# Attention and a routed FFN on one core: token rows scattered to expert regions batch by batch

## The chip, the core and the metric

The kernel runs on one core of one Trainium2 chip. The core has a matrix engine (TensorE, PE in the profile), a vector engine (DVE), a scalar engine (ACT), GpSimd (POOL) and a sync engine (SP) that mostly issues transfers. Each engine runs its own instructions in order and waits on semaphores for the others. The metric is the time of one execution in device microseconds (us), as a median over runs.

## The reference

The computation has two halves. Blockwise causal attention runs on q, k and v of 8 batches, 8 heads, 576 positions and 64 columns, with blocks of 64: a position sees its own block and all earlier ones. The heads are joined to x of 8 x 576 rows of 512. Then each row goes through one of 8 experts:

```
for s in range(S):
    fresh_e = argmax(logits[b, s])            # logits = x @ w_gate
    e = fresh_e if s == 0 or local_gate[b, s] < 0.5 else prev_e
    prev_e = e
    p = softmax(logits[b, s])
    out[b, s] = p[e] * (relu(x[b, s] @ w1[e]) @ w2[e])
```

The local gate is a sigmoid of x @ w_local. The expert of a token so depends on the token before it, within its batch: a scan along the sequence. w1 is 512 x 1024 and w2 is 1024 x 512 for each expert.

## The kernel before

Attention goes over 32 head pairs, four for each batch. Its loop (L607) is software pipelined: pass i turns the probabilities of pair i (`turn_p`, L519, PE transposes L526, evacuated by ACT or DVE at L541), makes scores of pair i + 1 (`scores`, L492) with row maxima on DVE (L508) and exponentials on ACT (L516), transposes q and k of pair i + 2 (`turn`, L471 to L478), finishes pair i - 1 (`finish`, L569), and multiplies by v (`attend`, L553). `pin` keeps the instructions of an engine in the order of the program. Loads are issued by SP for pair i + 3, except k of the first two pairs, which ACT issues; the columns of w_gate and w_local are loaded into `wg` from ACT's queue as well (L459, L460). `inverse` (L560) makes the inverse row sums `rv` by six DVE reciprocals. `finish` multiplies the attention output by `wg`, which holds an identity and the gate columns, so one matmul (L578) gives rows of x and their logits; DVE scales both by `rv`; POOL adds the logits into `lg_all` (L590, L591); SP writes the rows of x to HBM as `x_rows` (L593, L594). POOL also issues the loads of the expert weights, 16 of 1 MB, one after the other behind certain pairs.

`routing` (L145) is a generator. `routing(0)` handles batches 0 to 5 and takes one step at fixed points of pairs 24 to 31:

```
MIDDLE = {25: 1, 28: 1, 29: 1, 30: 1, 31: 2}
BEHIND = {24: 1, 25: 1, 26: 1, 27: 1, 28: 1, 29: 1, 30: 1, 31: 2}
```

Its steps: the argmax; a PE transpose (L188) and a round trip through HBM that lays the tokens of a batch in a row (L191, L193); the scan (L202); the way back (L204, L206, matmul L210); one-hot experts; ranks by matmuls with a triangular and a full matrix of ones (L225); the number of 128-token tiles of each expert; and, for each batch, one-hot matrices of slots (`hot`, L330, five POOL multiplies at L343) multiplied on PE (`add`, L350) to invert "token to slot" into tables: the token numbers that a tile gathers (`tok_g`), those that it writes (`tok_s`) and the probabilities (`pslot`). Steps left over at pair 31 run after the loop.

The FFN has 43 tiles of 128 tokens, each of one expert: 20 from the first six batches and 23 for all that is left. `gather` (L665, POOL) fetches rows of `x_rows` by `tok_g` with a bounds check; `turn_x` (L674) transposes them, DVE evacuates (`xb`, L677); `fetch` (L691) copies the expert's w1 into `wt` on DVE; `up` (L700) multiplies, with relu on ACT (L707) or, for the second half of a tile from tile 18 on, on DVE (L709); `down` (L714) multiplies by w2; ACT scales by the probability (L719); and POOL scatters the rows to the output (L720) with a bounds check. In program order tile t + 1's `up` is ahead of tile t's `down`. `routing(1)` repeats the routing for the last two batches and builds the tables of the last 23 tiles from all eight, one step per tile, on DVE.

## Time and profile before

| what | us |
|---|---|
| median of 3 runs (624.21 to 625.07) | 624.47 |
| the profiled execution | 625.85 |
| its span in the trace | 623.8 |
| PE busy | 563.6 |
| DVE busy | 452.7 |
| ACT busy | 329.4 |
| POOL busy | 155.3 |
| one head pair, pairs 2 to 24 | 11.90 |
| first up matmul of the FFN at | 429.81 |
| last tile's up matmuls at | 605.23 |

Times inside the trace count from the start of the span. The mean clock granted to PE was 0.975 of full speed. The costliest single groups are the exponentials (L516, 158.3 us on ACT), the row maxima (L508, 134.5 us on DVE) and the probability transposes (L526, 105.1 us on PE). A line such as "12.34 0.49 DVE L478 COPY kT<-ps_t" reads: start, duration, engine, line of the kernel, operation, output and input; what stands in brackets is the engine's idle time before it and what ended it.

### The profile page before, as it was taken

The page shows a single profiled execution, that of the slowest core. Times are in us where ns is not written, and L with a number is a line of the kernel's source. Part 1 is how long each engine was busy: PE and PEld are TensorE (multiplying, and loading weights), DVE is VectorE, ACT ScalarE, POOL GpSimd, SP SyncE. Part 2 cuts the span into 40 slices and gives each one's busy share as a digit, 9 for nine tenths or more (in the row PEclk, how much of TensorE's full clock was granted, in tenths as well). Part 3 has the DMA queues.
Part 4 walks back from the last instruction along what each step waited for, and adds up shares of the span by engine and source line. Part 5 has one row for each costly group of instructions (what it writes and reads, how often), then busy time and mean ns, then how long its engine had stood idle before and what let it go on. Part 6 is the DMA issues. An engine that isn't in the chain of part 4 may idle for free. (4 is left out here: it accounts for less than half of the span.)

```text
span 623.8 us, 15804 instructions
## 1 busy us (share of the span) xinstructions
PE 563.6 (90%) x5586; PEld 396.2 (64%) x5586; DVE 452.7 (73%) x1403; ACT 329.4 (53%) x1057; POOL 155.3 (25%) x218
## 2 busy tenths in 40 slices
PE   2899999999999999999999998765989899999991
PEld 1567667677677677666766665554667677766660
DVE  1688888888888888888888788894588855555540
ACT  1676676666666676666666765601444343323320
POOL 3000010010000001001010010144565565666532
PEclk9999999999999999999999999986999999999996
DMA  8246596595958668695874746102232222222210
GB/s 165 55 96 115 116 158 117 120 177 102 170 123 158 103 131 163 114 182 109 153 136 96 136 90 113 23 10 61 78 104 77 99 89 78 94 91 90 82 56 0
DMA packets 154078, 65.99 MB, mean 106 GB/s; under 512 B 138010, under 2 KB 146226, under 8 KB 154002
## 3 DMA queue, kind: packets, MB, share of 16 engines
q0 software_dynamic: 18048, 31.86, 24.8%
q1 hardware_dynamic: 132466, 32.52, 24.2%
q10 hardware_dynamic: 3488, 0.61, 0.6%
q8 instruction: 46, 0.75, 0.5%
q14 instruction: 30, 0.25, 0.1%
HBM read 67.55 MB, written 16.02 MB: 134 GB/s over the span
## 5 line engine op out<-in xcount | busy, mean ns | idle before, releaser
L516 ACT ACTIVATE pb<-ps_s,nm 128x512 f32<-128x512 f32 (+4 forms) x320 | 158.3, 501 | 97.8 <-DVE nm L508 97.3
L508 DVE TENSOR_REDUCE nm<-ps_s 128x1 f32<-128x512 f32 (+4 forms) x320 | 134.5, 453 | 54.0 <-ACT pb L516 31.8
L526 PE MATMUL ps_p<-id_f,pb 128*128 128x128 f32 (+1 forms) x800 | 105.1, 282 | 11.4 <-ACT pb L516 8.0
L492 PE MATMUL ps_s<-kT,qT 64*64 64x512 f32 (+7 forms) x1280 | 100.7, 419 | 6.1 <-ACT qT L475 6.1
L526 PEld LDWEIGHTS ps_p<-id_f,pb 128*128 128x128 f32 (+1 forms) x800 | 86.3, 141 | 24.7 <-ACT pb L516 10.0
L590 POOL TENSOR_TENSOR tmp<-tmp 128x45 f32<-128x45 f32 x32 | 8.5, 264 | 356.9 <-DVE tmp L582 356.9
L700 PEld LDWEIGHTS <-wt 128*128 128x128 bf16 x1376 | 81.1, 98 | 21.1 <-issue 15.8
L553 PE MATMUL ps_o<-pt,vt 128*64 128x320 f32 (+4 forms) x896 | 93.6, 360 | 0.0
L700 PE MATMUL ps_h<-xb,wt 128*128 128x128 bf16 x1376 | 84.3, 220 | 9.3 <-DVE xb L677 9.1
L714 PE MATMUL ps_o<-w_bf,hT 128*128 x344 | 86.6, 379 | 0.4
L553 PEld LDWEIGHTS ps_o<-pt,vt 128*64 128x64 f32 x896 | 59.3, 137 | 35.8 <-DVE tmp L582 4.9
L707 ACT ACTIVATE hT<-ps_h 128x512 bf16<-128x512 f32 x61 | 36.4, 597 | 79.1 <-PE ps_h L700 79.1
L720 POOL DMA_INDIRECT out_dram<-o_sb,tok_s x43 | 54.5, 1268 | 63.8 <-DMA out_dram<-o_sb,tok_s 21.0
L492 PEld LDWEIGHTS ps_s<-kT,qT 64*64 64x64 f32 x1280 | 45.4, 134 | 38.2 <-issue 23.6
L691 DVE COPY wt<-w_bf 128x4096 bf16 x43 | 53.1, 1238 | 15.5 <-PE ps_h L700 13.0
L516 ACT ACTIVATION_READ_ACCUMULATOR pb<-ps_s,nm 128x1 f32 x320 | 64.3, 201 | 0.0
L665 POOL DMA_INDIRECT xg<-x_rows,tok_g x43 | 55.3, 1286 | 22.6 <-PE ps_x L674 9.3
L719 ACT ACTIVATE o_sb<-ps_o,pslot 128x512 f32<-128x512 f32 x43 | 29.5, 687 | 44.0 <-PE ps_o L714 38.3
L709 DVE TENSOR_SCALAR hT<-ps_h 128x512 bf16<-128x512 f32 x25 | 17.3, 691 | 48.1 <-PE ps_h L700 48.1
L578 PE MATMUL ps_n<-wg,ot 128*128 128x146 f32 x320 | 49.4, 303 | 0.0
L541 ACT COPY pt<-ps_p 64x128 f32<-64x128 f32 (+2 forms) x102 | 43.6, 441 | 10.5 <-PE ps_p L526 10.3
L714 PEld LDWEIGHTS <-hT 128*128 128x128 bf16 x344 | 31.2, 98 | 24.8 <-issue 1.1
(147 smaller groups left out, 568.7 us busy)
## 6 DMA issues: line engine op xcount, KB each, us to landing
w_bf<-in_moe_w_dram POOLq DMA_DIRECT2D x16, 1024.0 KB, 10.2
natq<-in_q_dram SPq DMA_DIRECT2D x64, 128.0 KB, 2.6
vt<-in_v_dram SPq DMA_DIRECT2D x64, 128.0 KB, 4.7
natk<-in_k_dram SPq DMA_DIRECT2D x60, 128.0 KB, 2.7
x_rows<-xt SPq DMA_DIRECT2D x32, 128.0 KB, 2.6
natq<-in_q_dram SPq DMA_DIRECT2D x32, 32.0 KB, 2.5
vt<-in_v_dram SPq DMA_DIRECT2D x32, 32.0 KB, 6.3
natk<-in_k_dram SPq DMA_DIRECT2D x30, 32.0 KB, 2.2
```

Of the source, the lines that this page charges most:

```text
L492: pin(nc.tensor.matmul(ps[y][f * 64:(f + 1) * 64, c:c + n], lhsT=qT[r, i * 64:(i + 1) * 64], rhs=kT[r, a:a + n], start=True, stop=True))
L508: pin(nc.vector.reduce_max(nm[:, z:z + 1], ps[g][y][:, c:c + n], axis=AX, negate=True))
L516: pin(nc.scalar.activation(pb[i][:, a:a + n], ps[g][y][:, c:c + n], func=AF.Exp, bias=nm[:, i:i + 1], accum_out=rs[:, z:z + 1]))
L526: pin(nc.tensor.transpose(ps[:kk, (c + e) * P:(c + e + 1) * P], pb[i0 + 2 * e][:, j * P:j * P + kk], id128))
L541: pin(cp(dst, src))
L553: pin(nc.tensor.matmul(ps[h * D:(h + 1) * D, a - q0:qn], lhsT=vts[i % 3][:, j, h, :], rhs=pt[j][:, h, a - j * P:a - j * P + n], start=(j = ...
L578: pin(nc.tensor.matmul(ps[:, (t - t0) * (P + WG):(t - t0 + 1) * (P + WG)], lhsT=ot[:, t * P:(t + 1) * P], rhs=wg[:, hp], start=True, stop= ...
L665: nc.gpsimd.indirect_dma_start(out=xg[:], out_offset=None, in_=x_dram[:rows], in_offset=bass.IndirectOffsetOnAxis(ap=tok_gs[k][:, u:u + 1] ...
L691: nc.vector.tensor_copy(wt.rearrange("p k f -> p (k f)"), w1_bf[:, bass.ds(o, WE)])
L700: nc.tensor.matmul(ps_h[:, f, :], lhsT=wt[:, ko, fo * P:(fo + 1) * P], rhs=xb[:, ko * P:(ko + 1) * P], start=(ko == 0), stop=(ko == KO1 - 1))
L714: nc.tensor.matmul(ps_o, lhsT=hT[:, fo, :], rhs=w2_bf[:, bass.ds(woff + fo * Dm, Dm)], start=(fo == 0), stop=(fo == FO - 1))
L720: nc.gpsimd.indirect_dma_start(out=out_flat, out_offset=bass.IndirectOffsetOnAxis(ap=tok_ss[k][:, u:u + 1], axis=0), in_=o_sb[:], in_offse ...
```

## The change

- Rows are kept per batch in SBUF, as 258 words: 512 bf16 values of x, the token's number and its probability. After a batch's routing, five indirect transfers scatter them to `x_sorted`, where each expert owns a region of 4608 rows. Each transfer writes through a view of its own, declared disjoint from the others. Rows past the end of a batch go to spare rows.
- `routing(b)` now handles one batch and has eight steps, at (pair, part) points given by `hook`: part 0 is after the transposes of the probabilities, 1 before the third group of scores, 2 at the end of a pass. Batches 0 to 6 run inside attention, batch 7 in the FFN. A running count `K.free` gives each expert's next free row.
- The tables come from the counts alone (`table`): `table(0)` for 16 tiles in pair 28, `table(1)` for 27 tiles in the FFN. Slots, one-hot inversions, `tok_s` and `pslot` are gone; the token's number and probability come with the gathered row.
- Three tiles are gathered at the end of pass 29, the other 13 of the first part behind the last pair's gate logits.
- Gathers have no bounds check; output scatters write through disjoint views and have one only for the last seven tiles.
- One DVE reciprocal and six POOL copies take the place of six reciprocals; `wg` and k of pair 1 are loaded by SP; a one-element exponential stands at the start of ACT; v has two buffers for three and is loaded for pair i + 2 instead of i + 3; the evacuations of the probabilities have one pattern for all pairs; DVE takes the second relu from tile 14 on.

The diff, cut to its core:

```diff
-    lg_all = w_p.tile([P, B * NJ, E + 1], F32, tag="lg_all", name="lg_all")
-    x_dram = nc.dram_tensor("x_rows", [BS, Dm], BF16).ap()
+    ROW = Dm // 2 + 2
+    xs = nc.dram_tensor("x_sorted", [E * BS + B * P, ROW], I32).ap()
+    xs_views = dram_disjoint_views(xs, B * NJ)
+    out_views = dram_disjoint_views(out_flat, NT)
+    PARTS = [NB0 * S // P - E - 3, 0]
+    PARTS[1] = NT - PARTS[0]
...
+    TILES = [(k, u) for k in range(2) for u in range(PARTS[k])]
+    def gather(t, xg):
+        k, u = TILES[t]
+        nc.gpsimd.indirect_dma_start(
+            out=xg[:], out_offset=None, in_=xs,
+            in_offset=bass.IndirectOffsetOnAxis(ap=rows[k][:, u:u + 1], axis=0))
+        return xg
+    EARLY = 3
+    xgs = []
+    def gather_early():
+        for t in range(EARLY):
+            xgs.append(gather(t, rt([P, ROW], I32, "x_first", bufs=EARLY)))
+    def new_batch():
+        x = rt([P, NJ, ROW], I32, "x_b", bufs=2)
+        lg = rt([P, NJ, E + 1], F32, "lg", bufs=2)
+        return x, lg
+    def routing(b, x, lg, psum, pin, ew):
+        full = [P, NJ, E]
+        mx = rt([P, NJ], F32, "mx")
+        pin(dve.reduce_max(mx, lg[:, :, :E], axis=AX))
+        mx3 = mx[:, :, None].to_broadcast(full)
+        eqm = rt(full, F32, "eqm")
+        pin(dve.tensor_tensor(eqm, lg[:, :, :E], mx3, op=ALU.is_ge))
+        pin(ew.tensor_mul(eqm, eqm, K.desc[:, None, :].to_broadcast(full)))
+        ep = rt(full, F32, "ep")
+        pin(ew.tensor_sub(ep, lg[:, :, :E], mx3))
+        pin(pool.iota(x[:, :, Dm // 2:Dm // 2 + 1], pattern=[[P, NJ], [0, 1]],
+                      base=b * S, channel_multiplier=1))
+        yield
+        best = rt([P, NJ], F32, "best")
+        pin(dve.reduce_max(best, eqm, axis=AX))
+        ak = rt([P, 2, NJ], F32, "ak")
+        pin(dve.tensor_single_scalar(ak[:, 1, :], lg[:, :, E], 0.0, op=ALU.is_ge))
+        pin(dve.memset(ak[0:1, 1, 0:1], 0.0))
+        fresh = rt([P, NJ], F32, "fresh")
+        pin(dve.tensor_scalar(fresh, ak[:, 1, :], -1.0, 1.0, op0=ALU.mult, op1=ALU.add))
+        pin(dve.scalar_tensor_tensor(ak[:, 0, :], best, -float(E), fresh,
+                                     op0=ALU.add, op1=ALU.mult))
+        pin(nc.scalar.activation(ep, ep, func=AF.Exp))
+        yield
+        ps = psum()
+        pin(nc.tensor.transpose(ps[:2 * NJ, :P], ak.rearrange("p a c -> p (a c)"), id_f))
+        akT = rt([2 * NJ, P], BF16, "akT")
+        pin(nc.scalar.copy(akT, ps[:2 * NJ, :P]))
+        a_dram = nc.dram_tensor("a_dram%d" % b, [2, NJ * P], BF16).ap()
+        nc.sync.dma_start(out=a_dram.rearrange("a (t p) -> (a t) p", p=P), in_=akT)
+        row = rt([1, 2, NJ * P], BF16, "row")
+        nc.sync.dma_start(out=row, in_=a_dram.rearrange("(o a) s -> o a s", o=1))
+        sm = rt([P, NJ], F32, "sm")
+        pin(dve.reduce_sum(sm, ep, axis=AX))
+        yield
+        pin(dve.reciprocal(sm, sm))
+        pin(dve.tensor_tensor_scan(row[:, 0, :S], row[:, 1, :S], row[:, 0, :S], 0.0,
+                                   op0=ALU.mult, op1=ALU.add))
+        e_dram = nc.dram_tensor("e_dram%d" % b, [1, NJ * P], BF16).ap()
+        nc.sync.dma_start(out=e_dram, in_=row[:, 0, :])
+        ecr = rt([NJ, P], BF16, "ecr")
+        nc.sync.dma_start(out=ecr, in_=e_dram.rearrange("o (t p) -> (o t) p", p=P))
+        yield
+        ps = psum()
+        pin(nc.tensor.matmul(ps[:, :NJ], lhsT=ecr, rhs=K.id_b[:NJ, :NJ], start=True, stop=True))
+        oh = rt(full, BF16, "oh")
+        pin(dve.tensor_tensor(oh, ps[:, :NJ, None].to_broadcast(full),
+                              K.niota[:, None, :].to_broadcast(full), op=ALU.is_equal))
+        pin(dve.memset(oh[64:, NJ - 1:, :], 0.0))
+        cum = rt([P, NJ + 1, E], BF16, "cum")
+        pin(ew.memset(cum[:, 0:1, :], 0.0))
+        for c in range(NJ):
+            pin(ew.tensor_add(cum[:, c + 1, :], cum[:, c, :], oh[:, c, :]))
+        pin(ew.tensor_mul(ep, ep, oh))
+        yield
+        ps = psum()
+        n = NJ * E
+        pin(nc.tensor.matmul(ps[:, :n], lhsT=K.tri_b, rhs=oh.rearrange("p c e -> p (c e)"),
+                             start=True, stop=False))
+        pin(nc.tensor.matmul(ps[:, :n], lhsT=K.ones_b,
+                             rhs=cum[:, :NJ].rearrange("p c e -> p (c e)"),
+                             start=False, stop=True))
+        pin(nc.tensor.matmul(ps[:, n:n + E], lhsT=K.ones_b, rhs=cum[:, NJ, :],
+                             start=True, stop=True))
+        rk = rt([P, NJ + 1, E], F32, "rk")
+        pin(nc.scalar.copy(rk.rearrange("p c e -> p (c e)"), ps[:, :n + E]))
+        pg = rt([P, NJ], F32, "pg")
+        pin(dve.reduce_sum(pg, ep, axis=AX))
+        pin(dve.tensor_mul(x.bitcast(F32)[:, :, Dm // 2 + 1], pg, sm))
+        yield
+        pin(dve.tensor_add(rk[:, :NJ], rk[:, :NJ], K.free[:, None, :].to_broadcast(full)))
+        pin(dve.tensor_mul(rk[:, :NJ], rk[:, :NJ], oh))
+        to = rt([P, NJ], F32, "to")
+        pin(dve.reduce_sum(to, rk[:, :NJ], axis=AX))
+        to_i = rt([P, NJ], I32, "to_i", bufs=2)
+        pin(dve.tensor_copy(to_i, to))
+        pin(dve.tensor_copy(to_i[64:, NJ - 1:], K.spare[64:, b:b + 1]))
+        pin(dve.tensor_add(K.free, K.free, rk[:, NJ]))
+        yield
+        for c in range(NJ):
+            pin(pool.indirect_dma_start(
+                out=xs_views[b * NJ + c], out_offset=bass.IndirectOffsetOnAxis(ap=to_i[:, c:c + 1], axis=0),
+                in_=x[:, c, :], in_offset=None))
+        yield
+    def table(k, pin):
+        nt = PARTS[k]
...
+        pin(dve.tensor_sub(cnt, K.free, K.first))
+        if k == 1:
+            pin(dve.tensor_sub(cnt, cnt, K.taken))
+            ts(cnt, cnt, 1.0, float(P - 1))
+        pin(dve.tensor_copy(ci[:, 0], cnt))
+        pin(dve.tensor_single_scalar(ci[:, 1], ci[:, 0], 7, op=ALU.arith_shift_right))
+        pin(dve.tensor_copy(til, ci[:, 1]))
+        pin(dve.tensor_tensor_scan(end, K.ones_e, til, 0.0, op0=ALU.mult, op1=ALU.add))
+        pin(dve.tensor_sub(exc, end, til))
+        ts(a, exc, -float(P), K.part[:, 0:1])
+        pin(dve.tensor_add(a, a, K.first))
+        yield
+        no = rt([P, nt], F32, "no")
         if k == 0:
+            pin(dve.tensor_copy(no, K.tile_no[:, :nt]))
+            lim = small("lim")
...
+        else:
+            pin(dve.tensor_add(a, a, K.taken))
+            last = rt([P, 1], F32, "last")
+            ts(last, end[:, E - 1:], 1.0, -1.0)
...
+            pin(dve.tensor_scalar(no, K.tile_no[:, :nt], last[:, 0:1], 0.0,
+                                  op0=ALU.min, op1=ALU.add))
...
+        ge = rt(full, F32, "ge", tag="big")
+        pin(dve.tensor_tensor(ge, no[:, :, None].to_broadcast(full),
+                              end[:, None, :].to_broadcast(full), op=ALU.is_ge))
+        te = rt([1, nt], F32, "te")
+        pin(dve.reduce_sum(te, ge[0:1], axis=AX))
+        ts(te_is[k], te, float(WE), 0.0)
+        yield
+        prod = rt(full, F32, "prod", tag="prod")
+        def pick(out, f, name):
+            d = small(name)
+            pin(dve.memset(d[:, E - 1:], 0.0))
+            pin(dve.tensor_sub(d[:, :E - 1], f[:, 1:], f[:, :E - 1]))
+            pin(dve.tensor_mul(prod, ge, d[:, None, :].to_broadcast(full)))
+            pin(dve.reduce_sum(out, prod, axis=AX))
+            ts(out, out, f[:, 0:1], 0.0, op0=ALU.add)
+        r = rt([P, nt], F32, "r")
+        pick(r, a, "d_a")
+        pin(dve.scalar_tensor_tensor(r, no, float(P), r, op0=ALU.mult, op1=ALU.add))
+        if k == 1:
...
+            pin(dve.tensor_tensor(r, r, rc, op=ALU.min))
+        pin(dve.tensor_copy(rows[k], r))
...
-        vts = [cst.tile([P, NJ, 2, D], F32, tag="v%d" % x, name="vt") for x in range(3)]
+        vts = [cst.tile([P, NJ, 2, D], F32, tag="v%d" % x, name="vt") for x in range(2)]
...
-                eng = nc.scalar if nm == "k" and i < 2 else nc.sync
+                eng = nc.scalar if nm == "k" and i == 0 else nc.sync
...
+        warm = rt([P, 1], F32, "warm")
+        nc.vector.memset(warm, 0.0)
+        pin(nc.scalar.activation(warm, warm, func=AF.Exp))
...
-            nc.scalar.dma_start(out=wg[r, :, c:c + E], in_=gsrc[h])
-            nc.scalar.dma_start(out=wg[r, :, c + E:c + E + 1], in_=lsrc[h])
+            nc.sync.dma_start(out=wg[r, :, c:c + E], in_=gsrc[h])
+            nc.sync.dma_start(out=wg[r, :, c + E:c + E + 1], in_=lsrc[h])
...
+            pin(nc.vector.reciprocal(rs[:, :NB], rs[:, :NB]))
             for f in range(2):
                 r = slice(f * 64, (f + 1) * 64)
-                pin(nc.vector.reciprocal(rv[:64, 0:1, f ^ swap[0]], rs[r, 0:1]))
-                pin(nc.vector.reciprocal(rv[:64, 1:, f ^ swap[2]], rs[r, 2:NB:2]))
-                pin(nc.vector.reciprocal(rv[64:, :NJ - 1, f ^ swap[1]], rs[r, 1:NB:2]))
+                pin(nc.gpsimd.tensor_copy(rv[:64, 0:1, f ^ swap[0]], rs[r, 0:1]))
+                pin(nc.gpsimd.tensor_copy(rv[:64, 1:, f ^ swap[2]], rs[r, 2:NB:2]))
+                pin(nc.gpsimd.tensor_copy(rv[64:, :NJ - 1, f ^ swap[1]], rs[r, 1:NB:2]))
...
-            r = x_dram[b * S:(b + 1) * S, hp * P:(hp + 1) * P]
-            nc.sync.dma_start(out=r[:S4].rearrange("(t p) d -> p t d", p=P), in_=xt[:, 0:4, :])
-            nc.sync.dma_start(out=r[S4:], in_=xt[:S - S4, 4, :])
+            first, second = tmp[:, :, 0], tmp[:, :, 1]
+            last = pin(nc.gpsimd.tensor_add(lg if hp == 0 else first, first, second))
+            if hp > 0:
+                last = pin(nc.gpsimd.tensor_add(lg, lg, first))
...
+        def plan(steps, at):
+            for a in at:
+                todo.setdefault(a, []).append(steps)
+        def hook(i, part):
+            if part == 2 and i % HP == 0 and i > 0:
+                b = i // HP - 1
+                steps[b] = routing(b, *batches[b], psum, pin, pool)
+                plan(steps[b], [(i, 2), (i + 1, 0), (i + 1, 1), (i + 2, 0), (i + 2, 2),
+                                (i + 3, 1), (i + 3, 2), (i + 3, 2)])
+                if b == NB0 - 1:
+                    plan(table(0, pin), [(i + 4, 0), (i + 4, 1), (i + 4, 2)])
+            for x in reversed(todo.get((i, part), ())):
+                next(x, None)
+            if (i, part) == (HP * NB0 + HP + 1, 2):
+                gather_early()
...
-                engines = ("dve", "act", "dve", "act", "act", "act" if 24 < i < 31 else "dve", "act")
-                for u, eng in enumerate(engines):
+                for u, eng in enumerate(("dve", "act", "dve", "act", "act", "dve", "act")):
                     turn_p(u, eng)
+            hook(i, 0)
...
-            for _ in range(MIDDLE.get(i, 0)):
-                next(steps)
+            hook(i, 1)
...
-                attend(i, 1)
+                pv_last = attend(i, 1)
                 inverse(rss[i])
             if i + 3 < NPR:
-                nats[i + 3] = load(i + 3)
-            for _ in range(BEHIND.get(i, 0)):
-                next(steps)
-        for _ in steps:
-            pass
-        finish(NPR - 1)
+                nats[i + 3] = load(i + 3, "qk")
+            if i + 2 < NPR and i >= 0:
+                load(i + 2, "v")
+            hook(i, 2)
+        gate_last = finish(NPR - 1)
...
-            if n == 0 or t < NT0 - 2:
+            if n == 0 or t < N0 - 2:
...
+            tok = xgs[t][:, Dm // 2:Dm // 2 + 1]
+            if t >= NCT:
+                tok_e = f_p.tile([P, 1], I32, tag="tok_e", name="tok_e")
+                nc.gpsimd.tensor_tensor(tok_e, tok, skip_i[:, t - NCT:t - NCT + 1], op=ALU.add)
+                tok = tok_e
...
             nc.gpsimd.indirect_dma_start(
+                out=out_views[t],
+                out_offset=bass.IndirectOffsetOnAxis(ap=tok, axis=0),
+                **({"bounds_check": BS - 1, "oob_is_err": False} if t >= NCT else {}))
...
+        def gather_next():
+            t = len(xgs)
+            xgs.append(gather(t, x_p.tile([P, ROW], I32, tag="xg", name="xg")))
+        with tc.issue_after(gate_last.ins):
+            while len(xgs) < N0:
+                gather_next()
...
+        def late_steps():
+            for b in range(NB0, B):
+                if b not in steps:
+                    steps[b] = routing(b, *batches[b], psum, lambda x: x, dve)
+                yield from steps[b]
+            yield from table(1, lambda x: x)
+        late = late_steps()
...
+                with tc.issue_after(pv_last.ins):
+                    xb = turn_x(xgs[t])
...
-            for _ in range(1 if t < 8 or t % 2 else 2):
-                next(steps, None)
-            if t + ahead < NT:
-                xgs.append(gather(t + ahead))
+            for _ in range(2 if t < 6 else 1):
+                next(late, None)
+            while len(xgs) < min(NT, t + ahead + 1):
+                if len(xgs) == N0:
+                    for _ in late:
+                        pass
+                gather_next()
```

## The prediction

> **What bounds the kernel now.** I read the slices of the page first, then the busy times by stretch with one stretch per head pair, then the timeline at each joint. Page, slices of the span (digits are tenths):
>
> ```profile
> PE   2899999999999999999999998765989899999991
> DVE  1688888888888888888888788894588855555540
> PEclk9999999999999999999999999986999999999996
> ```
>
> PE is full but for the start, a dip around slices 25–28 and the end: the end is set by PE plus these gaps. Stretches (busy time and instructions by engine, granted clock, DMA):
>
> ```profile
> core 0: us, PE busy (x) PEld busy (x) DVE busy (x) ACT busy (x) POOL busy (x), PEclk, DMA share, GB/s
> 201.14:213.04 11.90, 11.90 (x117) 8.31 (x113) 10.02 (x36) 8.02 (x29) 1.40 (x3) 1.00 0.47 90
> ...
> 332.70:345.44 12.74, 12.21 (x114) 8.29 (x114) 9.77 (x34) 9.18 (x35) 1.44 (x3) 1.00 0.41 84
> ...
> 358.47:372.22 13.75, 12.37 (x116) 8.42 (x116) 11.04 (x40) 8.72 (x32) 2.10 (x4) 1.00 0.41 76
> ...
> 386.81:401.91 15.10, 12.49 (x103) 8.59 (x104) 12.80 (x44) 8.25 (x31) 2.13 (x7) 0.89 0.37 63
> ...
> 411.10:429.81 18.71, 5.51 (x38) 4.46 (x39) 12.96 (x54) 0.27 (x1) 8.64 (x14) 0.60 0.10 26
> 429.81:506.93 77.12, 71.63 (x829) 53.27 (x828) 56.03 (x151) 32.97 (x55) 45.04 (x36) 0.99 0.26 86
> 506.93:605.23 98.30, 92.68 (x1055) 66.91 (x1054) 51.45 (x71) 30.79 (x48) 55.46 (x44) 1.00 0.26 86
> ```
>
> A quiet pair takes 11.90 us, all of it PE; pairs 25–30, which carry routing, take 12.56, 12.74, 13.03, 13.75, 14.59 and 15.10. From 411.10 to the first up matmul at 429.81 PE works 5.51 of 18.71 us: DVE builds tables. Timeline, at the start, where the FFN begins, in the first routing of the FFN, and at the end:
>
> ```profile
> 7.81 0.49 DVE L478 COPY kT<-ps_t 128x320 f32<-128x320 f32 x1 [0.30 <-PE ps_t L471]
> ...
> 11.81 1.28 ACT L475 ACT_TABLE_LOAD   x1 [11.81 <-DMA wg<-in_moe_w_gate_dram]
> ...
> 13.86 3.69 PE L492 MATMUL ps_s<-kT,qT 64*64 64x512 f32 x20 [6.09 <-ACT qT L475]
> ...
> 429.81 4.78 PE L700 MATMUL ps_h<-xb,wt 128*128 128x128 bf16 x64
> ...
> 440.71 0.24 ACT L190 CAST akT<-ps_g 20x128 bf16<-20x128 f32 x1
> ...
> 445.40 1.35 DVE L202 TENSOR_TENSOR_SCAN erow<-row 2x576 bf16<-2x576 bf16 x1 [0.76 <-DMA row<-a_dram]
> ...
> 449.79 0.18 PE L210 MATMUL ps_g<-id_b,ecr 10*128 10x10 bf16 x1 [0.34 <-DMA ecr<-e_dram]
> ...
> 610.50 0.69 ACT L719 ACTIVATE o_sb<-ps_o,pslot 128x512 f32<-128x512 f32 x1 [1.04 <-PE ps_o L714]
> 610.75 0.98 POOL L720 DMA_INDIRECT out_dram<-o_sb,tok_s  x1 [1.89 <-DMA out_dram<-o_sb,tok_s]
> ...
> 613.60 0.98 POOL L720 DMA_INDIRECT out_dram<-o_sb,tok_s  x1 [1.87 <-issue]
> ...
> 616.45 0.98 POOL L720 DMA_INDIRECT out_dram<-o_sb,tok_s  x1 [1.87 <-DMA out_dram<-o_sb,tok_s]
> ```
>
> At the start ACT sits behind its weight-gate transfers until 11.81, and PE waits 6.09 us for qT. At the end the last rows are ready at 611.19, but each scatter waits 1.9 us for the one before it, and the last is issued at 616.45.
>
> **The sum**, against the profiled execution's 625.85 us (span 623.8); the median of the runs, 624.47, is 1.38 lower, taken off at the end.
>
> *1. Start.* The gate weights leave ACT's queue and the table load comes early, so qT no longer waits. kT is ready at 7.81 + 0.49 = 8.30; scores start there, not at 13.86: −5.5. Bounds −6.5 and −4.5 (a microsecond for natk and gate weights, which now share SP's queue). The removed memset of the logits was under this wait.
>
> *2. Routing of batches 0–6 inside attention.* Each batch adds five PE instructions, two ACT copies, some 20 DVE operations, POOL work and five 128-row scatters, spread over four pairs. PE, in order and full, pays its own instructions (L210's kind, 0.18 each: 0.9) plus the 0.3 a DVE scan of 1.35 can hold back the next evacuation beyond DVE's 11.90 − 10.02 = 1.88 free; about 1.25 a batch, 8.75 for seven, and 0.25 for the first table in pair 28: +9. The reciprocals, six per pair down to one on DVE with six copies on POOL, give DVE back 2 × (0.153 + 0.165 + 0.174) − 0.21 = 0.77 us per pair; PE sets the period, so that is worth nothing. The copies queue on POOL behind at most five scatter issues (5 × 1.27 = 6.35 of 11.90): under cover. The two gate additions and rows written to HBM pair by pair vanish from POOL and SP: nothing. SP now waits inside its queue for the landing of the routing's rows (2 to 3 us each, by 4.69 for two, below); the loads behind it are for two or three pairs ahead, so nothing, and 3 us a wait if that lead were gone. The third buffer of v goes; its load, issued after the attend that frees the buffer, has a pair (11.9) against a landing of 4.7 to 6.3. Bounds: own PE time of L201 and L224 alone, +2, and 0.65 on each of 28 pairs, two thirds of the 1.03 by which pair 28 exceeds pair 26, +18.
>
> *3. The dip of pairs 25–30 goes.* Excess over 11.90 in 25 to 29: 0.66 + 0.84 + 1.13 + 1.85 + 2.69 = 7.2. Pair 30, 15.10, loses its routing, its stall and the clock of 0.89 and comes to about 11.3: 3.8 more. −11.0 (−9 to −12; what routing still stands there is in step 2).
>
> *4. Last pair to first up matmul.* From pair 31's start (401.91) it is 27.9 us now. After: probability transposes 3.2, the wait for their last evacuation 0.6, the matmuls of pair 30's finish and of routing 1.9, attend 2.93: 8.6; then on DVE, in order, ot 0.6, reciprocal 0.3, four rank operations 0.9 (0.22 each, the pace of small ones at 451.30), weight copy 1.23, 0.3, the four multiplies of the last finish 1.36, second weight copy 1.2, xb 0.42: 6.3, 15.1 with the gaps. The first rows were gathered in pair 29, so nothing waits for tables, whereas now a gather follows them (landing 3.3). −12.8 (−8 if a gather still waits for all scatters of batch 6; −14.5 if PE goes ahead of the multiplies).
>
> *5. FFN, first to last up.* Now 77.12 + 98.30 = 175.4. After, batch 7 alone runs here, and the inversion matrices of both routings are gone; its chain is short but early. Up 0 and 1 take 4.78, down 0 1.9, and the cast of akT comes at 6.9. From that cast to the scan is 4.69 now, from the scan to L210 4.39, so the one-hot matmul, in order on PE, comes at 16.0 while PE's work before it ends at 11.6: a stall of 4.4. Eight DVE operations at 0.22 bring up 3 to 17.8. Then 22 small operations (4.8), a weight copy 1.23 and xb 0.42 on DVE: up 4 at 24.3. Ten more, four of them on 27 × 8 columns (0.45 each by 0.29 for 80 columns): up 5 at 28.9. Then nine undisturbed tiles of 3.77 (the period at 440.93) to up 14 at 62.8. From tile 14, no longer 18, the second relu is DVE's, and relu, weight copy and xb in this order give 4.27 (the period of most tiles now): 28 × 4.27 − 0.5 = 119.1. Sum 181.9; the clock falls again in the stall, 4.78 against 3.56: 1.2. 183.1: +7.7 (0 if DVE orders around the stall, +14 if 29 of the small operations take twice 0.22). Gathers of larger rows (1032 bytes for 1024), 13 of them 1.29 apart on POOL, stay ahead of the tiles.
>
> *6. End.* The scatters no longer wait on each other: the last follows its rows at 611.3 instead of 616.45: −5.1 (−3 to −5.7).
>
> −5.5 + 9 − 11.0 − 12.8 + 7.7 − 5.1 = −17.7; 625.85 − 17.7 − 1.38 = **606.8**.
>
> One rule against a row, which the sum does not need. The clock was granted at 0.60 over the idle 18.71 us above, and the first 64 up matmuls took 4.78 instead of the 3.56 that 64 take later: 1.2 us per gap. The Trainium skill, "TensorE: Matmul & The Clock Gate", Part 1, has half rate after an idle window of about 3.4 us, and full rate only after as long a busy one. By it a stall of 4.4 us would cost an estimated 1.7, and the sum would be 607.3. I keep the row.
>
> **Rivals.**
> - *The steps fit.* The routing rides in DVE's 1.88 spare us and costs PE only its few matmuls (+2), and the FFN's chain loses 3 less: 606.8 − 7 − 3 = 596.8. For: pair 26 shows few DVE operations at 9.77 busy. Against: pair 28.
> - *The steps are dearer*, +18 for +9: 615.8. For: two steps share some pairs. Against: no single step has more than about seven DVE operations.
> - *Slower.* Pair 28 has ten routing operations on DVE and takes 1.03 more than pair 26, which has nearly none. If each of the 28 pairs with steps pays this, step 2 is 28.8, not 9: 626.6. It takes all of the gain at (17.7 + 9)/28 = 0.95 us a pair. For: DVE there is 11.04 busy, the most a pair can hold before PE's order slips. Against: new DVE steps are spread, some four operations each, and the reciprocals leave 0.77.
> - *The change does not do what it says*: gathers are still held by late scatters to the sorted rows, so step 4 is worth nothing: 619.6. The early gathers are issued before batch 7 scatters, which speaks against it.
>
> **How the numbers follow.** Likeliest 0.52; steps fit 0.17; dearer 0.16; slower 0.12; not as said 0.03. The likeliest's own range, 600 to 615, comes from adding one or two bounds of steps 2, 4 and 5. From both neighbours I take most, so the range is 594 to 623; outside are the slower case (above) and the cheapest sums. 0.2% is 1.25 us and about what can be told from no change. Faster: 0.52 + 0.17, 0.15 of the dearer case and 0.02 of the last: 0.86. Within 0.2%: 0.02, the rest of those two. Slower: 0.12.
>
> **What would show it.** Step 1: first scores before 9 us. Step 2: pairs of 12.0 to 12.6, with PE's idle time before evacuations released by DVE. Pairs at 12.9 or more make the slower rival. Step 3: at most one slice below 9 between 24 and 28. Step 4: some 15 us from the last pair's first transpose to the first up matmul, ended by DVE's xb. Step 5: a stall near 4 us ended by the ecr transfer and periods of 4.27 after tile 14. Step 6: scatters not ended by an earlier one. Wrong would be: POOL's reciprocal copies late behind scatters, shown by waits of DVE's multiplies for rv; SP's loads late, shown by PE waits for natq.

## The result: 639.28 us, 2.4% slower

The changed kernel takes 639.28 us (median of 4 runs, 638.92 to 640.69) against 624.34 for the kernel before beside it. The ratio is 1.0243, with a 95% interval of 1.0224 to 1.0263. Forecast were 606.8 us and a range of 594 to 623, with a chance of 0.12 for slower. The span of the profiled execution grew by 13.9 us, from 623.8 to 637.7. Cut at the same five places, the two traces say where (joints are first instructions on TensorE):

| stretch | before | after | moved | forecast |
|---|---|---|---|---|
| start to first transposes of pair 0 | 23.55 | 17.36 | −6.2 | −5.5 |
| pair 0 to pair 31 | 378.36 | 377.63 | −0.7 | −2.0 (+9 − 11.0) |
| pair 31 to first up matmul | 27.90 | 14.68 | −13.2 | −12.8 |
| first to last tile's up matmuls | 175.42 | 211.23 | +35.8 | +7.7 |
| from there to the end | 18.57 | 16.80 | −1.8 | −5.1 |

Four of the five stand within 3.3 us of the forecast. All that was lost, and more than was gained elsewhere, is in the FFN. The profile's slices of the changed kernel (digits are tenths) show it at the right:

```profile
PE   5999999999999999999999989679986887777992
DVE  3678788888888888888888887547434443433540
PEclk9899999999999999999999999788999998988997
```

The dip in the middle is short now, but TensorE is busy for 0.6 to 0.8 of the slices where it was at 0.9 before. Busy times by stretch of the changed kernel, first a quiet pair, a pair with five scatters, then the last pair to the first up matmul, and the FFN up to tile 11, from tile 11 to 34 and from 34 to 42 (columns: stretch, its length, busy time and instructions of each engine, granted clock, DMA share and rate):

```profile
core 0: us, PE busy (x) PEld busy (x) DVE busy (x) ACT busy (x) POOL busy (x), PEclk, DMA share, GB/s
53.35:65.06 11.71, 11.71 (x116) 8.37 (x114) 9.40 (x31) 7.92 (x29) 1.52 (x8) 1.00 0.84 162
112.92:125.12 12.20, 12.04 (x118) 8.32 (x114) 10.37 (x37) 8.24 (x31) 7.39 (x14) 1.00 0.52 129
...
394.99:409.67 14.68, 9.38 (x86) 7.83 (x86) 10.91 (x39) 2.98 (x12) 7.62 (x24) 0.93 0.05 19
409.67:461.46 51.79, 47.44 (x480) 35.78 (x480) 27.56 (x80) 19.68 (x34) 39.66 (x35) 0.86 0.31 96
461.46:587.70 126.24, 98.24 (x1015) 72.91 (x1014) 48.27 (x66) 29.16 (x50) 56.70 (x52) 0.93 0.24 79
587.70:620.90 33.20, 30.31 (x348) 21.93 (x348) 16.22 (x23) 10.23 (x16) 10.22 (x11) 1.00 0.13 49
```

The first eleven tiles took 51.79 us. The forecast's own terms for them (28.9 to tile 5, then six of 3.77) make 51.5, the stall for batch 7 included (its parts hit less well, see below). Tiles 34 to 42 run at 4.27 or less, as forecast. Tiles 11 to 34 took 126.24, where the forecast's terms make 96.7 (tile 14 at 62.8 less 51.5, and 20 × 4.27): **29.5 us in 23 tiles**, in which no engine is busy for more than 98.24 us. The groups and the waits of ACT in this kernel name the wait (busy us and mean ns, idle time before, what ended most of it; and in the second line the total, number and longest of one kind of wait):

```profile
L709 ACT ACTIVATE o_sb<-ps_o,xg 128x512 f32<-128x512 f32 x40 | 27.5, 687 | 107.3 <-DMA out_dram<-o_sb,xg 89.0
```

```profile
ACT o_sb L709 <- DMA out_dram<-o_sb,xg: 89.0, 21, 5.5
```

ACT waits for output scatters to land, 21 times, once in each tile from 9 to 30 but one. There was no such wait before. ACT and GpSimd in two of these tiles:

```profile
464.35 0.69 ACT L709 ACTIVATE o_sb<-ps_o,xg 128x512 f32<-128x512 f32 x1 [4.07 <-DMA out_dram<-o_sb,xg]
464.93 1.07 ACT L693 ACTIVATE hT<-ps_h 128x512 bf16<-128x512 f32 x2
469.12 0.69 ACT L709 ACTIVATE o_sb<-ps_o,xg 128x512 f32<-128x512 f32 x1 [3.11 <-DMA out_dram<-o_sb,xg]
```

```profile
459.70 1.38 POOL L710 DMA_INDIRECT out_dram<-o_sb,xg  x1 [0.30 <-ACT hT L693]
464.98 0.98 POOL L149 DMA_INDIRECT xg<-x_sorted,rows  x1 [3.90 <-PE ps_x L660]
466.27 0.99 POOL L710 DMA_INDIRECT out_dram<-o_sb,xg  x1 [0.30 <-ACT hT L693]
469.74 1.03 POOL L149 DMA_INDIRECT xg<-x_sorted,rows  x1 [2.48 <-PE ps_o L700]
471.07 0.99 POOL L710 DMA_INDIRECT out_dram<-o_sb,xg  x1 [0.30 <-ACT hT L693]
```

GpSimd is idle for 2.5 to 3.9 us before each of these gathers, though the gather fetches rows that nobody needs soon: counted along the queue, the scatter issued at 459.70 is tile 5's and the gather at 464.98 is tile 22's. PE had long read what the profile names, so it is another wait. In two later turns the profile names it itself, the landing of a scatter:

```profile
539.62 0.98 POOL L149 DMA_INDIRECT xg<-x_sorted,rows  x1 [2.52 <-DMA out_dram<-o_sb,xg]
562.66 0.98 POOL L149 DMA_INDIRECT xg<-x_sorted,rows  x1 [2.42 <-DMA out_dram<-o_sb,xg]
```

In the program's order the gather of tile t + 17 takes the buffer that tile t's gathered rows were in (the pool has 17), and since the change those rows hold the token numbers that tile t's output scatter reads. So the gather waits for that scatter to land, and the scatter of tile t + 1 stands behind the gather on GpSimd's queue. One turn is landing, gather, scatter: from the scatter at 459.70 to that of tile 26 at 575.02 it took 115.3 / 21 = 5.5 us a tile, against the 4.27 of the other engines. From tile 6 to 26 scatters run 16 to 19 us behind their rows. The output rows have four buffers, so ACT waits for the scatter of four tiles ago, and TensorE waits for the relus that stand behind that on ACT. From tile 26 on no gather is left, and the scatters catch up at once. The median landing of a scatter was 2.9 us here and 2.8 before: the scatters are not slow, they are waited for one by one. The Trainium skill, "DMA: Bandwidth & Descriptors", "Anatomy of one DMA — SWDGE (gpsimd) path", gives 2.0 us plus the bytes over 436e3 per us for a transfer issued by GpSimd, which for 256 KB makes an estimate of 2.6; the measured landings are near it.

### The profile page after: what moved, and what is told of

Its sections match the earlier page's. It is cut to its first block, busy times and chain, and to the rows that moved or that the text cites. A ratio compares the mean times of both kernels' runs of the same rounds, so it can differ in the third digit from the quotient of the medians.

```text
span 637.7 us, 15811 instructions
## 1 busy us (share of the span) xinstructions
PE 569.8 (89%) x5548; PEld 405.6 (64%) x5548; DVE 423.3 (66%) x1269; ACT 322.4 (51%) x1054; POOL 223.8 (35%) x496
## 5 line engine op out<-in xcount | busy, mean ns | idle before, releaser
L700 PE MATMUL ps_o<-w_bf,hT 128*128 x344 | 89.6, 386 | 26.2 <-ACT hT L693 26.2
L686 PEld LDWEIGHTS <-wt 128*128 128x128 bf16 x1376 | 91.8, 106 | 23.4 <-issue 14.2
L686 PE MATMUL ps_h<-xb,wt 128*128 128x128 bf16 x1376 | 95.6, 234 | 10.6 <-DVE xb L663 10.4
L709 ACT ACTIVATE o_sb<-ps_o,xg 128x512 f32<-128x512 f32 x40 | 27.5, 687 | 107.3 <-DMA out_dram<-o_sb,xg 89.0
L695 DVE TENSOR_SCALAR hT<-ps_h 128x512 bf16<-128x512 f32 x29 | 20.1, 692 | 88.0 <-PE ps_h L686 88.0
L149 POOL DMA_INDIRECT xg<-x_sorted,rows x40 | 49.4, 1234 | 62.4 <-issue 19.8
L543 POOL COPY rv<-rs 64x1 f32<-64x1 f32 x64 | 11.9, 186 | 126.5 <-DVE rs L540 60.3
L693 ACT ACTIVATE hT<-ps_h 128x512 bf16<-128x512 f32 x57 | 33.4, 594 | 37.3 <-PE ps_h L686 33.9
L514 DVE COPY pt<-ps_p 128x64 f32<-128x64 f32 (+2 forms) x192 | 43.0, 283 | 10.7 <-PE ps_p L501 10.7
L516 ACT COPY pt<-ps_p 128x512 f32<-128x512 f32 (+2 forms) x96 | 41.5, 446 | 10.6 <-PE ps_p L501 10.6
```

The source lines that it names most:

```text
L149: nc.gpsimd.indirect_dma_start(out=xg[:], out_offset=None, in_=xs, in_offset=bass.IndirectOffsetOnAxis(ap=rows[k][:, u:u + 1], axis=0))
L514: pin(cp(dst[:, :, h], src[:, :, 1 - h]))
L516: pin(cp(dst, src))
L686: nc.tensor.matmul(ps_h[:, f, :], lhsT=wt[:, ko, fo * P:(fo + 1) * P], rhs=xb[:, ko * P:(ko + 1) * P], start=(ko == 0), stop=(ko == KO1 - 1))
L700: nc.tensor.matmul(ps_o, lhsT=hT[:, fo, :], rhs=w2_bf[:, bass.ds(woff + fo * Dm, Dm)], start=(fo == 0), stop=(fo == FO - 1))
```

## The experiments

The runs fell on different chips. The kernel before took 624.3 and 624.9 us (median) on two of them, and 630.5 to 631.9 on four others; I call these the quick and the slow chips. Ratios are always to the kernel before on the same chip.

**The changed kernel itself, again.** No edit.

> The changed kernel itself again, beside the next runs on one chip. In the first four experiments the kernel before took 630.6 us, not 624.3, and the traces show signals from TensorE that reached ACT and DVE 5 to 9 us late while GpSimd issued gathers or scatters one after the other; the changed kernel's own trace shows none. If that belongs to the chip, this run shows it where the kernel before is slow, and takes 655 to 665; where the kernel before takes 624, it takes 639.

Measured: 658.50 us on a slow chip, ratio 1.0431 (1.0382 to 1.0481); repeated on another, 658.80, 1.0454 (1.0422 to 1.0487). Against the quick chip's trace, pair 31 starts 17.6 us later (412.58 for 394.99): five of the six pairs with five scatters take 14.7 to 14.9, where the row above has 12.20, and the sixth, beside a table, 16.2. (Pair 18 has none and takes 15.4, and on the quick chip 13.2 where others in its place take 12.0; why is open.) The step from tile 2 to tile 3 takes 19.8 us for 9.3. So on slow chips a second loss is added that the first trace does not have. ACT's wait for scatters is absent here: its output buffers come free in time, since the tiles themselves are late. The loop on GpSimd is not absent. It stands for 2.5 us and more before nearly every far gather, and a turn takes mostly 4.8 us, as the tiles do:

```profile
515.32 1.02 POOL L149 DMA_INDIRECT xg<-x_sorted,rows  x1 [2.52 <-DMA out_dram<-o_sb,xg]
```

**Gathers behind scatters**, the loop taken out:

```diff
-                gather_next()
+                with tc.issue_after(scat[len(xgs) - 6].ins):
+                    gather_next()
```

> The changed kernel, with one edit: from tile 16 on, the gather of tile t is issued only behind the output scatter of tile t - 6, so that GpSimd's queue holds scatters ahead of far gathers. Nothing is left out. Theory (a loop on GpSimd's queue): in the changed kernel gathers stand 17 tiles ahead of the scatters in the queue; the gather of tile t + 17 needs the buffer that the scatter of tile t still reads its token numbers from, so it waits for that scatter's landing, and the scatter of tile t + 1 stands behind it. One turn of this loop took 5.5 us a tile from tile 5 to 26, more than the 4.27 of the other engines. Without it the periods from tile 12 on are 3.8 to 4.3, ACT does not wait for landings of scatters, and the time is about 611 (28 less than 639.3). Rival (contention): scatters that no longer wait for each other run beside the gathers and each lands later; then this edit leaves the landings and the time as they are, 635 to 640.

Measured: on slow chips only, 642.14 us (ratio 1.0159, 1.0101 to 1.0217), 646.88 beside the changed kernel's 658.50, and 646.78 beside 658.80. Tiles 11 to 34 take 102.67 instead of 110.22 beside it. GpSimd no longer stands before a gather (0.3 us each). The sign is that of the loop theory, but not the 28 us: 12 us beside the changed kernel. In the two traces 7.5 us are gained in these tiles and 7.2 ahead of them, where the edit also breaks up a row of gathers, and 3.5 are lost behind tile 34. A turn of the loop is shorter on these chips (4.8 us for 5.5) and the tiles without it are slower (4.4 for 4.27). What the loop costs on the quick chip these runs can't tell.

**Token numbers copied to a buffer of their own**, by ACT:

```diff
-            tok = xgs[t][:, Dm // 2:Dm // 2 + 1]
+            tok = f_p.tile([P, 1], I32, tag="tok_c", name="tok_c", bufs=NT)
+            nc.scalar.copy(tok, xgs[t][:, Dm // 2:Dm // 2 + 1])
```

> The changed kernel, with one edit: ACT copies the column of token numbers of each gathered tile to a small buffer of its own (43 of them), and the scatter reads the copy; the order of gathers and scatters on GpSimd's queue stays as the scheduler makes it. Nothing is left out. Loop theory: a row's buffer is free once PE and ACT have read it, gathers stop waiting for landings, and the time is 611 to 615 (the copies cost ACT about 0.2 us a tile, which it has). Rival (the far lead of the gathers itself, or contention, holds the scatters): 635 to 640.

Measured: 674.25 us, ratio 1.0708 (1.0656 to 1.076), the slowest of all. Expected wrongly. Waits of ACT and its lines in two tiles of this kernel:

```profile
ACT tok_c L704 <- DMA xg<-x_sorted,rows: 98.3, 34, 5.3
```

```profile
528.98 0.19 ACT L704 COPY tok_c<-xg 128x1 int32<-128x1 int32 x1 [5.30 <-DMA xg<-x_sorted,rows]
529.08 0.68 ACT L710 ACTIVATE o_sb<-ps_o,xg 128x512 f32<-128x512 f32 x1
...
534.18 0.19 ACT L704 COPY tok_c<-xg 128x1 int32<-128x1 int32 x1 [3.94 <-DMA xg<-x_sorted,rows]
534.27 0.68 ACT L710 ACTIVATE o_sb<-ps_o,xg 128x512 f32<-128x512 f32 x1
```

Scatters now follow their rows by 0.28 us, so the buffer was what had held them. But the scheduler puts the copy of a gather just issued ahead of the output rows on ACT, and ACT waits out that gather's landing in each tile: gather, landing, copy, output rows, scatter, next gather. The loop went through ACT instead.

**Scatters chained again**, and **seven buffers of output rows**:

```diff
-                out=out_views[t],
+                out=out_flat,
...
-                **({"bounds_check": BS - 1, "oob_is_err": False} if t >= NCT else {}))
+                bounds_check=BS - 1, oob_is_err=False)
```

```diff
-            o_sb = f_p.tile([P, Dm], F32, tag="o_sb", name="o_sb")
+            o_sb = f_p.tile([P, Dm], F32, tag="o_sb", name="o_sb", bufs=7)
```

> The changed kernel, with the output scatters as before the change: all through one view of the output, with a bounds check. Nothing is left out. Loop theory: the scatters are already kept apart by the loop, one landing each, so chaining them costs little until the loop ends near tile 27, then some 2.8 us a scatter for those that pile up: 639 to 650. Contention rival: landings shorten when scatters run alone, and the time falls to 611 to 625.

> The changed kernel, with seven buffers of output rows for four (and three each of two other tiles for four, to make room). Nothing is left out. Loop theory: the loop's own period (5.5 us) stays, since it does not pass through the output buffers, but ACT meets it three tiles later: at the end of the loop the tile that starts at 579 us is number 33, not 30, and that is worth 11.4 us: about 628. If the output buffers themselves were the limit, the loop would shorten and the whole 28 us would go: about 611. Contention rival: 635 to 640 or no clear change.

Measured: 656.25 (ratio 1.0422, 1.0371 to 1.0473) and 658.65 (1.046, 1.0409 to 1.0512), both on the slow chip of the first experiments, where the changed kernel itself was not run; on the two other slow chips it took 658.50 and 658.80. Neither moves the time clearly, so chaining gives nothing back there, which speaks against contention of unchained scatters. The 11 us expected of the buffers could not show, since ACT does not wait for them on a slow chip.

**Thirteen buffers of gathered rows** for seventeen.

> The changed kernel with 13 buffers of gathered rows for 17, the fewest that the first part needs. Nothing is left out. Loop theory: what closes the loop is the reuse of a buffer that a scatter still reads, whatever the lead; the gather then stands 13 tiles ahead, its turn is as long, and the time is that of the changed kernel within 6 us. If it were the length of the lead (more transfers under way) that cost the time, a lead of 13 would give back a quarter of it, 6 to 8 us.

Measured: 660.14, ratio 1.0467 (1.0436 to 1.0498), beside 658.80 for the changed kernel: no change, as the loop theory has it, and GpSimd's waits before gathers are still there. But on a slow chip the run without the loop gave back only 12 us, and the quarter of that which a shorter lead was to give, 3 us, is hardly more than the noise, so the run doesn't settle it against the length of the lead.

**Everything reordered on GpSimd.** The gathers behind scatters and the token sums of the last seven tiles behind the scatter before; the five scatters of a batch spread over four points; and, in the second run, the gathers of tiles 5 to 15 not in one row:

```diff
+            if c < 3 and b < 6:
+                yield
...
+                behind = scat[len(xgs) - 6] if len(xgs) >= N0 else upmm[len(xgs) - 4]
+                with tc.issue_after(behind.ins):
+                    gather_next()
...
+                with tc.issue_after(scat[t - 1].ins):
+                    nc.gpsimd.tensor_tensor(tok_e, tok, skip_i[:, t - NCT:t - NCT + 1], op=ALU.add)
```

> The changed kernel with gathers behind scatters (from tile 16 on), the token sums of the last seven tiles behind the scatter before, and the five scatters of each of batches 0 to 5 no longer issued in one row but at four points of one pair and a half. Nothing is left out. In the repeated run of the changed kernel, where the kernel before took 632, the pair with the five scatters took 14.7 to 14.9 us, against 12.2 in the changed kernel's own trace, where the kernel before took 624. If a row of issues is what delays TensorE's signals, spreading makes these pairs 12.2 to 12.5 again and is worth 12 to 15 us there; if each issue costs some 0.5 us wherever it stands, the same 2.6 us are found again over two pairs and the time stays at that of gathers behind scatters. Where the kernel before takes 624, both expect 614 to 620.

> The run before, and the gathers of tiles 5 to 15 each behind the first matmuls of the tile four earlier instead of thirteen in one row where the FFN begins. Nothing is left out. If a row of issues delays the signals, the step from tile 2 to tile 3 (9.3 us in the changed kernel's trace, 18 to 20 in the repeated run) is 9 to 11 on any chip; if not, it stays at 18. Where the kernel before takes 624: 612 to 620; where it takes 632: 615 to 635.

Measured, on a quick chip: 636.56 us (ratio 1.0188, 1.0094 to 1.0282) and 636.71 (1.0188, 1.0145 to 1.0231). The total misses, but the stretches part cleanly. Of the second run, a quiet pair, a spread pair, then the FFN to tile 11, tiles 11 to 34, and 34 to 42:

```profile
65.20:76.91 11.71, 11.71 (x117) 8.37 (x114) 9.40 (x31) 7.93 (x29) 2.46 (x9) 1.00 0.41 82
125.23:145.05 19.82, 13.90 (x118) 9.86 (x115) 10.56 (x39) 8.51 (x31) 3.86 (x12) 0.83 0.62 117
437.97:488.04 50.07, 44.40 (x473) 33.35 (x481) 27.29 (x80) 19.36 (x34) 34.61 (x30) 0.92 0.28 89
488.04:585.00 96.96, 88.86 (x1001) 64.38 (x1014) 48.34 (x66) 32.02 (x50) 50.88 (x49) 1.00 0.31 102
585.00:618.20 33.20, 30.05 (x344) 21.93 (x348) 16.22 (x23) 10.24 (x16) 13.80 (x18) 1.00 0.21 69
```

Tiles 11 to 34 take **96.96 us instead of 126.24**, on the number that the forecast's terms make (96.7), with scatters unchained and the gather beside them; the first run has 96.97. ACT's wait for scatters falls from 89.0 us to 4.2. This is the kind of chip and the place where the loss was, so the loop is shown as its cause, and contention is out. (The changed kernel itself was not run on this chip; its trace is from the other quick one.) What the run lost is in attention: pair 31 starts at 423.40, 28.4 us later than in the changed kernel. Three pairs like the one above lose 6.9 to 8.0 each, pair 29 loses 3.5, and pair 18, which has no scatter, 2.1. GpSimd in the pair above, and in pair 13, where no weight load stands just ahead of the scatter:

```profile
122.84 0.95 POOL L356 DMA_DIRECT2D w_bf<-in_moe_w_dram  x1
124.09 1.01 POOL L267 DMA_INDIRECT x_sorted<-x_b,to_i  x1 [0.30 <-issue]
...
134.12 0.18 POOL L545 COPY rv<-rs 64x1 f32<-64x1 f32 x1 [7.16 <-DMA x_sorted<-x_b,to_i]
...
179.28 0.99 POOL L267 DMA_INDIRECT x_sorted<-x_b,to_i  x1 [0.15 <-issue]
...
183.24 0.18 POOL L545 COPY rv<-rs 64x1 f32<-64x1 f32 x1
```

A spread scatter came to stand right behind the issue of a 1 MB weight load, landed some 10 us later, and GpSimd's queue stood for it; inverse row sums and the next batch's argmax came 7 us late. For all four pairs with scatters that lose time, a weight load is issued 1.1 to 1.3 us ahead of the scatter; for pair 13 there is none, the copy does not wait, and the pair takes 11.91. Why that copy waits for the scatter at all is not shown. The Trainium skill, same page, "SWDGE vs HWDGE vs iDMA", says that only one queue is allocated for such transfers; a scatter that waits out a weight load agrees with that. Without these 28.4 us the run would be at 608.3 (an estimate from the two traces: no run put the two together on a quick chip).

**All relus on ACT** in addition:

```diff
-            if n == 0 or t < N0 - 2:
+            if n == 0 or t < NT:
```

> The run before, with all relus on ACT. Nothing is left out. With the loop gone and few signals late, tiles from 14 on are free to run at 3.8 instead of 4.3: up to 14 us less than the run before. If the issues on GpSimd (a gather and a scatter for each tile) hold the tiles at 4.3 and more, as in the first run with all relus on ACT, the two are within 4 us.

Measured: 634.25, ratio 1.0142 (1.0102 to 1.0182), 2.5 us less than the run before it on the same chip. The tiles from 16 on take 4.20, not 3.8: the second expectation. A first such run on a slow chip (without the other orders) took 647.71 beside 646.88.

**The same orders without spreading.**

> The run before this one, and two more orders on GpSimd's queue: the gathers of tiles 5 to 15 each behind the first matmuls of the tile four earlier, and the token sums of the last seven tiles behind the scatter before. Nothing is left out. The same two edits took 180 us from the first to the last up matmul beside scatters spread in attention; with the attention of the changed kernel (first up matmul at 410) and 17 us behind the last one that makes 609 where the kernel before takes 624, which beats it; 635 to 645 where it takes 631, since the rows of scatters in attention stay.

Measured, on two slow chips: 647.33 (ratio 1.0244, 1.0205 to 1.0283) beside 658.80 for the changed kernel, and 642.17 (1.0192, 1.0147 to 1.0236). Better than the changed kernel on the first (it was not run on the second), and behind the kernel before on both. On a quick chip these orders alone were not run, so the 609 expected there stays open.

**Disjoint views for the output alone**, in the kernel before:

```diff
-                out=out_flat,
+                out=out_views[t],
```

> The kernel before, with one part of the change alone: output scatters through disjoint views (their bounds check stays), so that none waits for the one before it. Nothing is left out. Step 6 of the prediction: the last scatter is issued at 611 or 612, not 616.5, and the time falls by 3 to 5. Rival: GpSimd's drain after the last scatter (6.5 us after that issue in the kernel before, 9.3 in the changed one) grows by what the issue gains, and the time moves by less than 2.

Measured, on a slow chip: 630.99, ratio 0.9989 (0.9972 to 1.0006): no clear change. At the end the views do what step 6 says: the last scatter is issued 0.3 us behind its rows, for 5.3 in the trace of the kernel before, GpSimd's closing drain (the long instruction it ends the program with) is the same in both (6.77 and 6.75 us), and from the last tile's up matmuls to the end it is 13.6 us (613.99 to 627.6) for 18.6. That the whole gains nothing clear is not explained. Tiles run at 4.6 here, for 4.27 on the quick chip, which need not be the views' doing: in a slow chip's trace without them (the last experiment below) it is 184.8 us from the first to the last tile's up matmuls, here 184.4. The last scatter there comes 3.5 us behind its rows. The kernel before itself has a trace on the quick chip alone.

**The transfers by themselves**: 24 indirect transfers added to the kernel before.

```diff
+            if i >= 5 and i < 20 and i % 2 == 1:
+                for c in range(5 if i % 4 == 1 else 1):
+                    c = extra.pop(0)
+                    pin(nc.gpsimd.indirect_dma_start(
+                        out=scr_views[c], out_offset=bass.IndirectOffsetOnAxis(ap=lane[:, c:c + 1], axis=0),
+                        in_=id_f[:], in_offset=None))
```

> The kernel before with 24 added indirect transfers of 128 rows of 512 bytes to a scratch area, whose data nobody reads: five in one row at the end of passes 5, 9, 13 and 17, one at the end of passes 7, 11, 15 and 19. All else is left as it is. This measures the issues by themselves. A pair takes 11.90 without them. If each issue delays TensorE's signals by some 0.5 us, pairs with five take 14 to 14.6 and pairs with one 12.3 to 12.5; if only a row of them does, pairs with one stay at 11.9; if the scatters are not the cause, all stay at 11.9. Where the kernel before takes 624, all stay below 12.2.

> The kernel before with the 24 added indirect transfers whose data nobody reads, again. Where the kernel before took 625, no pair showed them (11.90 in all). Where it takes 631: if rows of indirect transfers delay TensorE's signals there, pairs with five of them take 14 to 14.6 and pairs with one 11.9 to 12.5; if the scatters of the changed kernel cost their 2.6 us by something else (their data, their waits, the routing around them), all stay at 11.90.

Measured, one execution each: 625.27 beside 624.91 on the quick chip, 654.74 beside 630.49 on a slow one. The pair with five of them and the pair after it, first on the quick chip, then on the slow one:

```profile
94.06:105.95 11.89, 11.89 (x117) 8.30 (x114) 10.01 (x36) 8.02 (x29) 4.39 (x7) 1.00 0.54 115
105.95:117.84 11.89, 11.89 (x117) 8.30 (x114) 10.01 (x36) 8.02 (x29) 1.55 (x3) 1.00 0.93 180
```

```profile
95.00:113.22 18.22, 14.43 (x117) 9.47 (x113) 10.33 (x36) 8.27 (x29) 4.40 (x7) 0.81 0.35 75
113.22:125.12 11.90, 11.90 (x117) 8.30 (x113) 10.02 (x36) 8.02 (x29) 1.55 (x3) 1.00 0.93 178
```

On the quick chip five in a row cost nothing; on the slow one they cost 5.0 to 6.7 us in the four pairs that have them (16.87 to 18.63 for 11.90). Single ones cost nothing on either. So the second loss is shown to come from rows of such transfers alone, with no data, routing or wait of the change. ACT in the pair of the slow chip:

```profile
100.28 0.65 ACT L540 COPY pt<-ps_p 128x256 f32<-128x256 f32 x2 [4.82 <-remote]
```

"remote" stands where no instruction of the trace ended the wait: what ACT waits for had long been done on TensorE by the records. The same copy waits 0.73 us on the quick chip. The wait ends 1.3 us after GpSimd has ended its fifth issue (99.01). Why these chips differ stays open.

## Why the prediction was wrong, step by step

1. *Start*: right. First scores at 8.56 us (forecast 8.30), −6.2 up to pair 0. Pair 0 loses 1.6 of it again (12.56 for 10.93, at a granted clock of 0.86 for 1.00).
2. *Routing in attention, and 3. the dip*: the sum was right within 1.3 us, but by parts that cancel, so in part by luck. A batch costs 0.20 + 0.51 + 0.30 + 0.47 = 1.5 over 11.71 in its four pairs, not 1.25; pairs 28 and 29, with the first table and the early gathers, take 14.30 and 13.52, about 3.5 us more than I had. Against that, "PE sets the period, so that is worth nothing" was wrong for the reciprocals: quiet pairs fell from 11.90 to 11.71. The probability transposes and DVE's first evacuation of them, in a quiet pair before (from 201.14) and after (from 53.35):

```profile
201.14 3.18 PE L526 MATMUL ps_p<-id_f,pb 128*128 128x128 f32 x25
202.81 0.69 DVE L541 COPY pt<-ps_p 128x512 f32<-128x512 f32 x1
```

```profile
53.35 3.00 PE L501 MATMUL ps_p<-id_f,pb 128*128 128x128 f32 x25
54.32 0.63 DVE L516 COPY pt<-ps_p 128x512 f32<-128x512 f32 x1
```

In the kernel before, that evacuation starts behind six reciprocals, 1.67 us into the pair for 0.97, and the transposes, which need its buffer, take 0.2 us longer; no other group of TensorE's changes. 31 × 0.19 is 5.9 us. This is read from the two traces; no run takes the reciprocals out alone. PE was full by its busy time, 11.90 of 11.90, but that time held such a wait. The two signs named for this step's failure did not show: DVE never waits for `rv` in attention, and TensorE waits for `natq` only at the start.
3. *Pair 31 to first up matmul*: right (14.68 for 15.1).
4. *FFN*: wrong, and this alone turned the sign. The failing step is the sentence on the gathers, "13 of them 1.29 apart on POOL, stay ahead of the tiles", with nothing on the ones after them: it put the wait for a gather's buffer, and what stands behind it, at nothing. It measured 29.5 us. I priced the order of DVE and TensorE tile by tile, but of GpSimd's queue only the issue time. I had not asked what frees the buffer that a far gather takes. The answer was new with the change: the token number moved into the gathered row, so the row now lives until its output scatter has read it. Up to tile 11 the step was right within 0.3 us, and again with the loop gone (96.96 for 96.7). The first of these is partly luck: the first two tiles' up matmuls took 3.57 us each, for 1.95 in later tiles, at a granted clock of 0.62, more than was priced; the stall for batch 7 was 2.7 us, not 4.4; tile 3 came at 19.9 for 17.8, and the tiles from 5 to 11 took 21.8 for 22.6.
5. *End*: half right. The last scatter follows its rows by 0.77 us, and in the kernel before, the views alone made the end 5 us shorter (13.6 for 18.6, on another chip). But GpSimd's closing drain grew from 6.75 us to 9.52, which is not in step 6. Its cause is open: it was 2.71 in the runs with 24 added transfers.

The rival for slower (1.03 us on each of 28 pairs; the two rows, 13.75 and 12.74, make 1.01) was not what happened on the quick chip. No rival named an engine's queue in which a far transfer blocks a near one.

## What to carry to other kernels

When a buffer gets a new reader, follow who frees it now, and look along the in-order queue for work that stands behind the next user of that buffer. A prefetch as deep as the pool is not free: once it waits, everything queued behind it waits too. A step that moves waits between queues should be priced for every queue it passes, and a busy share of 1.00 on TensorE does not mean that removing work elsewhere is worth nothing.

## What the runs showed of the chip

- Five indirect transfers in a row delay other engines by 5.0 to 6.7 us on one chip and by nothing on another; the kernel before differs by only 1% between such chips (624.9 and 630.5). A kernel with many of them should be timed on more than one chip: the changed kernel is 2.4% slower on a quick one and 4.3 to 4.5% on slow ones.
- On slow chips DVE hears late from TensorE while GpSimd issues. In the repeated changed kernel, tiles 14 to 27, the second relu starts 0.35 to 1.43 us after the last up matmul of its tile, and 0.45 to 0.72 after a GpSimd issue has ended; on the quick chip it is 0.11 us in every tile from 14 on.
- GpSimd's closing drain took 6.75, 9.52 and 2.71 us in kernels with 86, 126 and 110 indirect transfers: not in step with their number. Each figure came again on the other kind of chip (6.77, 9.52, 2.71).
